# A fused attention and gated feed-forward kernel on one core: another written order of its pieces, with other pages and banks, behind an unchanged front part

## The chip, the cores and the metric

The kernel runs on one core of a Trainium2 chip. The metric is the device time of one execution in microseconds, the median over several runs. The core has five engines with a queue of instructions each: PE multiplies matrices, DVE, ACT and POOL work on elements, and SP issues the transfers (DMA) between the chip's main memory and the core. Each engine takes its instructions in order. An instruction that waits for another engine or for a transfer holds up everything behind it in its own queue.

## The reference

Local tokens (8 batches of 512) attend to the 32 global tokens of their batch and to local tokens within 32 positions; global tokens attend to everything. The result, 4608 tokens of 512, goes through a norm and a gated feed-forward layer:

```python
out_g = sm(scale * q_g @ k_all.T) @ v_all                      # 8 x 8 heads, 32 queries, 544 keys
s_ll  = where(|i - j| <= 32, scale * q_l @ k_l.T, -1e9)        # 512 x 512 for each head
out_l = sm([scale * q_l @ k_g.T, s_ll]) @ v_all
x  = concat(out_g, out_l)                                      # 4608 tokens x 512
xn = x / sqrt(mean(x * x) + 1e-6) * rms_g
y  = (silu(xn @ w_gate) * (xn @ w_val)) @ w_out                # 512 -> 1536 -> 512
```

## The kernel before

**Tiles and stages.** Tokens are done in nine chunks, c = 0 to 8: eight of 512 tokens, the last one of 256. Each chunk has an attention stage (pieces L, V, S, M, E, N, F, D, T, A and those with a G in front for the global tokens), a norm (n) and the feed-forward products. A product of 32-bit values is made of 16-bit high and low parts, as three matmuls. From chunk 1 on, the products in front of the gate use a scheme of seven products in place of eight: `moe_pair(ch, g, parts, n)` forms group g, six groups to a chunk. Its products stand as pieces P0 to P41, P(7g) to P(7g+6) for group g, and each is 12 matmuls of 256 columns. Piece R with the same number (`rest`) takes the sum out of its PSUM bank: on DVE as `tensor_tensor` (bank plus an earlier part), or on ACT as a copy. Several products of a group add on to one bank (`onto`), so R must have read the bank before the next product adds to it: P6 adds to the bank that R3 reads, and P2 begins a bank of its own. Two R pieces fill one tile, `u`: R4 on ACT and R5 on DVE. The pieces t form the gate, `moe_out` forms the products behind it (O0 to O41) and their R pieces from R49 on, and the stores.

**Weights.** They are prepared once by chunk 0 and put into main memory (`wd`, `wa`, `wb`). Every chunk fetches them again in pieces w: `fetch(c, g, i)` brings up to 512 KB from `wd` for two of the seven products, and `fetch_out` brings `wa` or `wb` for O.

**What sets the order.** Nothing is scheduled at build time. Every instruction is recorded under a piece name, "chunk:step.number", and at the end the pieces are written out in the order of a table. The queue of each of the five engines is this order with the other engines' pieces left out. Every instruction is issued from line 2095 (in `Later`), so all rows of the profile have that line:

```python
    for name in ORDER.split() or list(plan):
        for call in plan.pop(name):
            call()
```

Two more tables, `PAGES` and `BANKS`, give the place of each tile: 43 pages of 128 x 1024 words (and 8 wide ones) and 8 PSUM banks, taken one after the other in the order in which the program asks for tiles.

```python
        at = next(page_at)            # tile_of: the next word of PAGES, "25a" = page 25, first quarter
        return banks[int(next(bank_at))]   # bank_of
```

A tile may only be written when everything that used its page before has finished; the waits for this are put in from the places. So a table with other places has other waits, even between instructions that stay where they were.

Of the kernel before, what the change touches and what calls it, by code (L numbers as in the profile page):

```python
# [92 lines left out]
0:e3.5 0:M5.0.2 0:I4.11.0 0:p5.0 0:I4.01.0 0:e5.3 0:M5.0.1 0:m12.1 0:e5.0 0:g11.0 0:b3.0 0:M5.1.1
0:q10.0 0:B4.0 0:d6.0 0:e5.4 0:g11.1 0:e5.1 0:I5.00.0 0:I5.01.0 0:m17.0 0:m15.0 0:b4.0 0:I5.10.0
0:B5.0 0:s12.0 0:a8.0 0:e5.2 0:I5.11.0 0:q11.0 0:W14.0 0:a9.0 0:s17.0 0:M5.1.3 0:l12.1 0:s15.0
0:d8.0 0:e4.5 0:V5.0 0:I6.00.0 0:I6.01.0 0:B6.0 0:I6.10.0 0:l17.0 0:I7.10.0 0:h3.0 0:p6.0 0:l17.1
0:W16.0 0:e6.0 0:h4.0 0:l15.0 0:W13.0 0:m13.0 0:s13.0 0:k13.0 0:g13.0 0:e6.1 0:e6.2 0:g13.1 0:E5.1.0
0:b5.0 0:I6.11.0 0:I7.00.0 0:I7.01.0 0:d9.0 0:a10.0 0:B7.0 0:I8.10.0 0:d10.0 0:g17.0 0:E4.0.0
# [23 lines left out]
1:N0/0+1.0 1:w0.4 1:w14.0 1:P5.0 1:M0/0+1.0 1:N2/0+1.0 1:N3/0+1.1 1:N1/0+1.0 1:w2.0 1:N3/0+1.0
1:F3/0+1.0 0:J1.1 1:M2/0+1.0 1:R5.0 1:N0/0+1.1 1:GL/1+1.0 1:N2/0+1.1 1:M1/0+1.1 1:N1/0+1.1 1:R9.0
1:D3/0+1.0 1:R6.0 1:D3/0+1.1 1:P6.0 1:P7.0 1:P16.0 1:P2.0 1:M1/0+1.0 1:E2/0+1.0 1:P10.0 1:E1/0+1.0
1:F1/0+1.0 1:E0/0+1.0 0:o3.0 1:R10.0 1:P14.0 1:w3.0 0:u0.0 1:P12.0 1:F2/0+1.0 1:T3/0+1.0 1:w5.0
1:w6.4 1:D2/0+1.0 1:P11.0 1:D1/0+1.0 1:R7.0 1:P3.0 1:D1/0+1.1 1:w8.0 1:P18.0 1:w9.0 1:F0/0+1.0
1:D0/0+1.0 1:R3.0 1:P17.0 1:T1/0+1.0 1:D2/0+1.1 1:T2/0+1.0 0:J1.2 1:D0/0+1.1 1:T0/0+1.0 1:R17.0
1:R18.0 1:w11.0 1:R8.0 1:P19.0 1:P13.0 0:J1.4 1:A/0+1.0 1:B/0+1.0 1:R19.0 1:R4.0 0:j1.0 1:P15.0
0:u1.0 1:R5.1 1:w24.1 1:w24.2 1:R13.0 1:P26.0 1:w24.4 1:w30.0 1:X/0+1.0 1:w1.0 1:R20.0 1:Y/0+1.1
1:w30.1 1:R14.0 1:w30.3 1:P32.0 1:P33.0 1:R15.0 1:R11.0 1:w24.3 1:w46.0 1:w15.0 1:GS/1+1.0  # L130
1:GM/1+1.0 1:w26.0 1:GM/1+1.1 1:Y/0+1.0 1:Y/0+1.2 1:w38.0 1:w17.0 1:R33.0 1:GN/1+1.0 1:P24.0
1:GN/1+1.1 1:GM/1+1.2 1:GN/1+1.2 1:P25.0 0:o2.1 1:P20.0 1:R25.0 1:w30.2 1:w30.4 1:R16.0 1:P27.0
1:w46.1 1:w46.3 1:P21.0 1:GT/1+1.2 1:P40.0 1:P41.0 1:w32.0 1:X/0+1.1 1:R34.0 1:R17.1 1:w33.0 1:R26.0
1:R21.1 1:R41.0 1:GT/1+1.0 1:R27.0 1:X/0+1.2 1:GT/1+1.3 0:o3.1 1:P22.0 1:w18.0 1:GT/1+1.1 1:L/2+1.0
1:R42.0 1:P28.0 1:S/2+1.0 1:w48.1 1:N0/2+1.0 1:M1/2+1.0 1:N1/2+1.1 1:N1/2+1.0 1:P34.0 1:M3/2+1.1
1:M1/2+1.1 1:w38.1 1:w38.2 1:E1/2+1.0 1:F1/2+1.0 1:V/2+1.0 1:M2/2+1.0 1:w46.2 1:M2/2+1.1 1:E2/2+1.0
1:w46.4 1:w38.4 1:Y/0+1.3 1:M0/2+1.0 1:R21.0 1:N3/2+1.0 1:N2/2+1.0 1:N3/2+1.1 1:w38.3 1:M0/2+1.1
1:w18.1 1:E0/2+1.0 1:N0/2+1.1 1:F0/2+1.0 1:R9.1 1:w27.0 2:GL/1+1.0 1:P29.0 2:w18.1 1:R29.0
1:M3/2+1.0 1:E3/2+1.0 1:F3/2+1.0 2:w18.2 1:P23.0 1:w18.2 1:w18.4 1:D0/2+1.0 1:P35.0 1:R30.0 1:P30.0
1:P66.0 1:P31.0 1:R22.0 1:P38.0 1:w29.0 1:P39.0 1:P42.0 1:N2/2+1.1 1:P43.0 1:P36.0 2:GV/1+1.0  # L140
1:R12.0 1:D3/2+1.0 1:GA/1+1.0 1:D0/2+1.1 1:R28.0 1:w18.3 1:R23.0 1:D3/2+1.1 1:T3/2+1.0 1:P37.0
1:F2/2+1.0 1:w20.0 1:R31.0 1:w21.0 1:R24.0 1:T0/2+1.0 1:R13.1 1:D1/2+1.0 1:P46.0 2:w20.1 1:w44.0
1:w46.5 1:D1/2+1.1 3:w4.0 1:w40.0 1:D2/2+1.0 1:GN/1+1.3 1:w41.0 1:R35.0 1:R37.0 1:R25.1 1:D2/2+1.1
1:R29.1 1:R43.0 1:R36.0 0:o1.1 1:R37.1 1:w42.0 1:P44.0 1:L/0+2.0 1:R38.0 1:R39.0 1:w48.0 1:P47.0
1:R40.0 1:R41.1 1:T2/2+1.0 1:w43.0 1:R32.0 1:T1/2+1.0 1:A/2+1.0 1:w49.0 1:w23.0 1:w45.0 2:w0.0
# [2190 lines left out]
```

## Time and profile before

| | |
|---|---|
| time, median of 3 runs | 891.72 us (890.53 to 891.75) |
| the profiled execution's own time | 892.29 us |
| its span in the trace | 890.5 us (1.8 us lie around it) |
| busy: PE, DVE, ACT, POOL | 97%, 80%, 63%, 31% of the span |
| PE in the chain that ended last | 85% |

PE is busy nearly all the time. Its idle time by stages, the waits in which it lies, and the time by which other engines and transfers are ahead of it are what is to be read in this profile.

### The profile page before, as it was taken

The numbers are of one execution on the slowest core, as the hardware profiler recorded it, in microseconds if no ns is written. First come the engines' busy times: TensorE is split into PE (matmuls) and PEld (weight loads), VectorE is DVE, ScalarE is ACT, GpSimd is POOL, SyncE is SP. The second block draws the span as 40 slices with busy tenths as digits, with TensorE's granted clock in tenths as the row PEclk, the third lists the DMA queues.
The fourth block names the chain that finished last, engine by engine and source line by source line (L and its number), as shares of the span: only waits on it lengthen the run. The fifth ranks groups of instructions, "written<-read, shape, count | busy, mean of one in ns | idle before, by whom it ended". The sixth has DMA issues, their size and how long they took to land.

```text
span 890.5 us, 28310 instructions
## 1 busy us (share of the span) xinstructions
PE 864.1 (97%) x11646; PEld 666.4 (75%) x11646; DVE 709.7 (80%) x1857; ACT 557.9 (63%) x1362; POOL 277.8 (31%) x255
## 2 busy tenths in 40 slices
PE   5599999999999999999999999999999999999998
PEld 4554455545548885588888888888888888888997
DVE  5999999798686776777886899688886798587576
ACT  6999993657344664557473876568575772545343
POOL 0000000024834475414531255123441344124414
PEclk9699999999999999999999999999999999999999
DMA  9995340488974997984697567968796759747671
GB/s 353 407 392 190 96 142 25 141 277 283 374 253 143 288 304 230 312 266 150 218 376 263 172 224 218 339 234 291 254 366 206 253 152 366 262 140 229 229 255 62
DMA packets 102737, 216.79 MB, mean 243 GB/s; under 512 B 8272, under 2 KB 34640, under 8 KB 102608
## 3 DMA queue, kind: packets, MB, share of 16 engines
q1 hardware_dynamic: 102176, 214.66, 70.9%
q8 instruction: 91, 1.49, 0.7%
q10 hardware_dynamic: 432, 0.33, 0.1%
q14 instruction: 38, 0.31, 0.1%
HBM read 187.96 MB, written 27.00 MB: 241 GB/s over the span
## 4 chain that ended last, share of the span: by engine, by line
PE 85%; DMA 3%; DVE 3%; issue 1%; ACT 1%; SPq 1%; POOL 0%; DVEq 0%; POOLq 0%; ACTq 0%
PE bank L2095 85%; DVE page L2095 3%; DMA wide<-wd 1%; DMA page<-in_vb_dram 1%; DMA page<-in_gv_dram 1%; ACT page L2095 1%; DMA wb<-page 1%; SPq L2095 1%; POOL page L2095 0%; DVE wide L2095 0%; DVE xg L2095 0%; DVE ws L2095 0%; DVE sm L2095 0%; DVE hs L2095 0%; DVE pow L2095 0%
## 5 line engine op out<-in xcount | busy, mean ns | idle before, releaser
L2095 PE MATMUL bank<-page,page 128*128 128x256 f16 (+7 forms) x8406 | 726.8, 277 | 16.4 <-ACT page L2095 8.0
L2095 PEld LDWEIGHTS <-page 128*128 128x128 f16 (+1 forms) x5568 | 515.7, 98 | 159.4 <-issue 7.6
L2095 POOL TENSOR_TENSOR page<-page,page 128x512 f16<-128x512 f32 (+5 forms) x163 | 180.0, 1122 | 286.4 <-ACT page L2095 236.1
L2095 DVE TENSOR_TENSOR page<-bank,page 128x512 f32<-128x512 f32 (+1 forms) x179 | 113.9, 649 | 64.2 <-PE bank L2095 37.5
L2095 ACT COPY page<-bank 128x512 f32<-128x512 f32 (+3 forms) x172 | 86.9, 529 | 111.2 <-PE bank L2095 100.0
L2095 ACT CAST page<-page 128x512 f16<-128x512 f32 (+2 forms) x144 | 109.0, 780 | 73.5 <-DVE page L2095 59.9
L2095 ACT ACTIVATE page<-page,sm 128x128 f32<-128x128 f32 x344 | 126.5, 391 | 26.7 <-DVE sm L2095 21.7
L2095 DVE TENSOR_TENSOR page<-page,page 128x256 f32<-128x256 f32 (+4 forms) x145 | 90.5, 636 | 9.0 <-ACT page L2095 7.0
L2095 POOL TENSOR_TENSOR page<-page,sm 128x512 f32<-128x512 f32 x22 | 25.5, 1167 | 208.9 <-DVE sm L2095 201.0
L2095 ACT ACTIVATE page<-page 128x512 f32<-128x512 f32 (+2 forms) x93 | 77.1, 907 | 9.6 <-DVE page L2095 7.2
L2095 DVE CUSTOM_DVE_ANT_0 page<-bank,page 128x128 f32<-128x128 f32 x248 | 60.3, 283 | 19.9 <-PE bank L2095 18.8
L2095 PEld LDWEIGHTS bank<-page,page 64*32 64x32 f32 (+4 forms) x3072 | 55.2, 113 | 24.5 <-issue 11.0
L2095 PE MATMUL bank<-wide,page 32*64 32x96 f32 (+6 forms) x2074 | 63.4, 266 | 1.3 <-DMA page<-in_vb_dram 1.3
L2095 ACT ACTIVATE page<-page,half_inv 128x512 f32<-128x512 f32 (+1 forms) x68 | 44.7, 686 | 23.9 <-DVE page L2095 19.3
L2095 DVE TENSOR_TENSOR page<-page 128x256 f32<-128x256 f32 (+3 forms) x110 | 57.1, 533 | 1.1 <-PE bank L2095 0.2
L2095 PE MATMUL bank<-page,wide 128*128 128x256 f16 (+4 forms) x500 | 56.9, 269 | 0.8 <-DMA wide<-wd 0.8
L2095 DVE SCALAR_TENSOR_TENSOR page<-page,page 128x512 f32<-128x512 f32 (+1 forms) x68 | 46.8, 702 | 12.7 <-ACT page L2095 12.7
L2095 DVE SCALAR_TENSOR_TENSOR page<-page,c_h,page 128x512 f32<-128x512 f32 (+1 forms) x73 | 51.8, 728 | 0.7
L2095 PEld LDWEIGHTS <-wide 128*128 128x128 f16 x450 | 41.6, 98 | 13.9 <-DMA wide<-wd 1.1
L2095 ACT ACTIVATION_READ_ACCUMULATOR page<-page,sm 128x1 f32 x248 | 46.8, 189 | 0.0
L2095 POOL TENSOR_TENSOR page<-wide,page 128x512 f16<-128x512 f32 (+2 forms) x25 | 27.4, 1105 | 45.4 <-ACT page L2095 43.3
L2095 PEld LDWEIGHTS bank<-wide,page 32*64 32x64 f32 (+2 forms) x1936 | 29.5, 129 | 6.8 <-issue 2.7
(156 smaller groups left out, 662.1 us busy)
## 6 DMA issues: line engine op xcount, KB each, us to landing
page<-wd SPq DMA_DIRECT2D x117, 512.0 KB, 6.9
page<-wb SPq DMA_DIRECT2D x36, 512.0 KB, 7.0
page<-in_w_in_dram SPq DMA_DIRECT2D x24, 512.0 KB, 9.3
page<-wa SPq DMA_DIRECT2D x23, 512.0 KB, 6.4
page<-wd SPq DMA_DIRECT2D x42, 256.0 KB, 5.3
page<-in_qkb_dram SPq DMA_DIRECT2D x23, 448.0 KB, 6.1
wide<-in_gkq_dram SPq DMA_DIRECT2D x16, 576.0 KB, 8.1
page<-in_vw_dram SPq DMA_DIRECT2D x16, 512.0 KB, 9.3
```

What stands on the lines that cost most here:

```text
L2095: return lambda *a, **k: write(self.engine, lambda: call(*a, **k))
```

## The change

Only the three tables change. The 3754 pieces and the instructions in them are the same. Of `ORDER` the first 261 pieces stay, and 3376 of the others stand in another position (the median piece moves by 10 positions). Of the 1198 entries in `PAGES` the first 51 are as they were and 1079 differ; of the 438 in `BANKS` the first 40 are as they were and 346 differ. By the trace of before, the first instruction that stands elsewhere comes on SP at 56.5 us, on PE at 61.4, on DVE at 62.6, on ACT at 63.4 and on POOL at 181.

```diff
 ORDER = """
...
-0:d3.0 0:p4.0 0:W15.0 0:s8.0 0:e4.0 0:e4.1 0:g8.1 0:e3.1 0:I2.10.0 0:l8.0 0:g8.0 0:b1.0 0:e1.5
...
-0:S5.0 0:m10.0 0:d4.0 0:I3.00.0 0:I3.10.0 0:a7.0 0:q9.0 0:h2.0 0:I3.11.0 0:M5.1.2 0:a5.0 0:e4.4
...
 PAGES = """
...
-17a 18a 10a 21a 14a 22a 11a 0a 13a 20a 9a 1a 17a 3c 16a 12a 9a 14a 19a 32c 10a 39a 33a 8a 32c 15a
+17a 18a 10a 21a 14a 22a 11a 0a 13a 20a 9a 1a 17a 3c 16a 12a 9a 14a 19a 32c 10a 23a 42a 8a 32c 15a
...
```

**Place 1: chunk 7, group 0, from P4 to P6.** In the lists below a row is an instruction: what it writes, an arrow, what it reads, and the elements. The second number in a name is only a running one: `page25_88` is page 25. DVE before: these are R15, R2, R8, R3, R9 and R5.

```order
L2095 TENSOR_TENSOR page8_71<-bank1_115,page8_71 128x512
L2095 TENSOR_TENSOR page42_105<-bank7_121,page42_105 128x512
L2095 TENSOR_TENSOR page29_92<-bank6_120,page29_92 128x512
L2095 TENSOR_TENSOR page6_69<-bank0_114,page42_105 128x2x256
L2095 TENSOR_TENSOR page13_76<-bank3_117,page13_76 128x512
L2095 TENSOR_TENSOR page11_74<-bank7_121,page33_96 128x2x256
```

DVE now: R15, R9, then R5 (page 25), R3 and R6's sum as one row (x2), and t7.

```order
L2095 TENSOR_TENSOR page34_97<-bank3_117,page34_97 128x512
L2095 TENSOR_TENSOR page39_102<-bank0_114,page39_102 128x512
L2095 TENSOR_TENSOR page25_88<-bank1_115,page7_70 128x2x256
L2095 TENSOR_TENSOR page0_63<-bank6_120,page1_64 128x2x256 x2
L2095 SCALAR_TENSOR_TENSOR page9_72<-page9_72,page25_88 128x512
```

PE now, at the same place: the last matmuls of P4 (weights in page 25) and the first of P6 (bank 6).

```order
L2095 LDWEIGHTS page25_88
L2095 MATMUL bank7_121<-page8_71,page25_88 128x256
L2095 LDWEIGHTS page25_88
L2095 MATMUL bank7_121<-page30_93,page25_88 128x256
L2095 LDWEIGHTS page31_94
L2095 MATMUL bank6_120<-page35_98,page31_94 128x256
```

The tile `u`, which R5 writes, has moved from page 11 to page 25, which holds the weights of P4 and P5; and R3, which reads the bank of P6 (bank 0 before, bank 6 now), has moved from two places ahead of R5 to the place behind it. P4 stands directly ahead of P6, as it did before.

**Place 2: the start of chunk 7, from P7 to P2.** PE's pieces there were P8 P0 P1 P14 P2 P9 P15 P3 P7 and are P1 P8 P0 P7 P15 P14 P2 P9. ACT before: two casts and the copy R8 (of bank 6), three casts, R1 (of bank 5), the exponentials of the global attention, two copies, and R7 last (of bank 4).

```order
L2095 COPY page13_76<-bank6_120 128x512
L2095 CAST page16_79<-page15_78 128x512
L2095 CAST page5_68<-page11_74 128x512
L2095 CAST page15_78<-page36_99 128x512
L2095 COPY page42_105<-bank5_119 128x512
L2095 ACTIVATE wide2_108,gsm6_53_214<-wide2_108,gsm6_53_214 128x544 x2
L2095 ACTIVATE gsm6_53_214<-gsm6_53_214 128x2
L2095 COPY page33_96<-bank0_114 128x512
L2095 COPY page8_71<-bank2_116 128x512
L2095 COPY page29_92<-bank4_118 128x512
```

ACT now: an exponential, R7 (of bank 4, the product P7), the second exponential and its sum, a cast, and R8 (of bank 2).

```order
L2095 ACTIVATE wide1_107,gsm6_53_214<-wide1_107,gsm6_53_214 128x544
L2095 COPY page41_104<-bank4_118 128x512
L2095 ACTIVATE wide1_107,gsm6_53_214<-wide1_107,gsm6_53_214 128x544
L2095 ACTIVATE gsm6_53_214<-gsm6_53_214 128x2
L2095 CAST page9_72<-page20_83 128x512
L2095 COPY page39_102<-bank2_116 128x512
```

DVE now: R8's sum (page 41 with bank 2) stands ahead of the norm piece 6:n52.0, which writes page 8, read by P2.

```order
L2095 ISA wide1_107,gsm6_53_214<-bank3_117,zeros_130,gsm6_53_214 128x272
L2095 ISA gsm6_53_214 128x1
L2095 TENSOR_TENSOR page41_104<-bank2_116,page41_104 128x512
L2095 TENSOR_TENSOR page8_71<-page34_97,page9_72 128x512
L2095 TENSOR_TENSOR page1_64<-bank1_115,page1_64 128x512
L2095 TENSOR_TENSOR page7_70<-bank7_121,page7_70 128x512
```

On both engines the copy and the sum of group 1 (R7 and R8) have moved ahead of what P2 needs; before, R8's sum came behind the norm's pieces and behind P2's own result.

**Place 3: chunk 6, the weights of P23.** SP before: 6:w13 is the fifth row, into page 17, with a store ahead of it.

```order
L2095 DMA page2_65<-wd2_154 128x2048
L2095 DMA page21_84<-wd3_155 128x2x1024
L2095 DMA page18_81<-wd4_156 128x2048
L2095 DMA out_0_dram<-wide3_109 128x2x512
L2095 DMA page17_80<-wd3_155 128x2x1024
L2095 DMA page14_77<-wd3_155 128x2x1024
```

SP now: 6:w13 is the fifth row, into page 18.

```order
L2095 DMA page4_67<-wd4_156 128x2x1024
L2095 DMA page10_73<-wd5_157 128x1024
L2095 DMA page33_96<-wd4_156 128x2048
L2095 DMA page37_100<-wa_158 128x2048
L2095 DMA page18_81<-wd3_155 128x2x1024
L2095 DMA page20_83<-wd3_155 128x2x1024
```

PE now: the last matmuls of 6:P18 read page 18, and S/2+1 (64 matmuls of 128 columns), P22 and P20 stand between them and 6:P23, which reads page 18 again.

```order
L2095 LDWEIGHTS page18_81
L2095 MATMUL bank0_114<-page6_69,page18_81 128x256
L2095 LDWEIGHTS page18_81
L2095 MATMUL bank0_114<-page6_69,page18_81 128x256
L2095 MATMUL bank5_119<-page20_83,page9_72 32x128
L2095 MATMUL bank7_121<-page20_83,page9_72 32x128
```

The transfer of P23's weights now has the page that P18 reads until shortly before; before, it had page 17, and the trace issued it at 670.6 us, where P23 began at 700.1.

## Rows read from the trace of the kernel before

**Rows 1.** The page's line of busy time by engine, and its line of the chain that ended last, by engine.

```profile
PE 864.1 (97%) x11646; PEld 666.4 (75%) x11646; DVE 709.7 (80%) x1857; ACT 557.9 (63%) x1362; POOL 277.8 (31%) x255
PE 85%; DMA 3%; DVE 3%; issue 1%; ACT 1%; SPq 1%; POOL 0%; DVEq 0%; POOLq 0%; ACTq 0%
```

**Rows 2.** Busy time of each engine in stretches of the span: from and to, the length, PE, weight loads, DVE, ACT, POOL (number of instructions), then PE's granted clock as a share of full speed, the busy share of the DMA engines, and GB/s.

```profile
50.00:75.00 25.00, 23.77 (x198) 11.48 (x197) 24.83 (x67) 24.90 (x43) 0.00 (x0) 1.00 1.00 382
75.00:125.00 50.00, 50.00 (x448) 25.50 (x447) 49.12 (x122) 49.77 (x97) 0.00 (x0) 1.00 0.40 129
125.00:175.00 50.00, 50.00 (x551) 27.52 (x550) 44.05 (x120) 28.36 (x73) 0.87 (x1) 1.00 0.21 64
175.00:300.00 125.00, 124.78 (x1626) 74.07 (x1624) 97.03 (x245) 64.28 (x178) 58.29 (x46) 1.00 0.81 264
300.00:325.00 25.00, 24.20 (x290) 21.32 (x289) 19.61 (x56) 19.27 (x58) 13.98 (x10) 1.00 0.91 298
...
375.00:400.00 25.00, 24.49 (x449) 21.81 (x452) 18.63 (x36) 13.84 (x26) 2.60 (x3) 1.00 0.85 270
...
425.00:450.00 25.00, 23.66 (x459) 20.70 (x459) 21.01 (x55) 12.72 (x19) 11.57 (x11) 1.00 0.78 262
450.00:600.00 150.00, 149.88 (x2218) 131.66 (x2217) 121.92 (x317) 99.97 (x270) 45.29 (x41) 1.00 0.76 259
600.00:700.00 100.00, 99.79 (x1561) 87.59 (x1559) 78.44 (x213) 67.17 (x179) 36.92 (x34) 1.00 0.79 271
...
775.00:875.00 100.00, 99.91 (x1319) 91.62 (x1317) 75.39 (x178) 50.07 (x98) 33.98 (x38) 1.00 0.61 205
875.00:890.50 15.50, 11.70 (x104) 9.72 (x101) 6.78 (x18) 2.97 (x6) 8.12 (x15) 0.98 0.18 69
```

**Rows 3.** PE in order of time at two places: start, length, instructions, and in brackets the idle time ahead with its releaser.

```profile
65.77 1.46 PE L2095 MATMUL bank<-page,page 64*32 64x128 f32 x63 [0.68 <-DVE page L2095]
433.65 1.09 PE L2095 MATMUL bank<-wide,page 32*64 32x256 f32 x46 [1.34 <-DMA page<-in_vb_dram]
```

**Rows 4.** The chain that ended last, in order of time: start, length, what.

```profile
301.45 8.02 DMA wide<-wd
309.52 66.64 PE bank L2095 x765
376.18 0.59 ACT page L2095
376.87 0.69 DVE page L2095
...
425.96 7.55 DMA page<-in_vb_dram
...
603.89 0.59 ACT page L2095
604.51 0.70 DVE page L2095
605.25 28.54 PE bank L2095 x429
...
875.93 10.95 PE bank L2095 x98
886.89 0.02 issue
886.91 0.48 DVE page L2095
```

**Rows 5.** PE and then DVE in order of time at place 1, columns as in rows 3.

```profile
762.76 9.44 PE L2095 MATMUL bank<-page,page 128*128 128x256 f16 x85
...
767.62 2.48 DVE L2095 TENSOR_TENSOR page<-bank,page 128x512 f32<-128x512 f32 x4 [1.88 <-ACT page L2095]
```

**Rows 6.** ACT in order of time at place 2.

```profile
757.06 1.66 ACT L2095 CAST page<-page 128x512 f16<-128x512 f32 x3
759.14 0.59 ACT L2095 COPY page<-bank 128x512 f32<-128x512 f32 x1 [0.42 <-PE bank L2095]
759.62 0.75 ACT L2095 ACTIVATE wide<-wide,gsm 128x544 f32<-128x544 f32 x1
760.27 0.19 ACT L2095 ACTIVATION_READ_ACCUMULATOR wide<-wide,gsm 128x1 f32 x1
760.36 0.74 ACT L2095 ACTIVATE wide<-wide,gsm 128x544 f32<-128x544 f32 x1
761.00 0.19 ACT L2095 ACTIVATION_READ_ACCUMULATOR wide<-wide,gsm 128x1 f32 x1
761.23 0.21 ACT L2095 ACTIVATE gsm<-gsm 128x2 f32<-128x2 f32 x1
761.34 1.05 ACT L2095 COPY page<-bank 128x512 f32<-128x512 f32 x2
```

**Rows 7.** Transfers: number, KB each, and the median us from issue to landing; over the whole span, then of those issued between 668 and 674 us, then between 690 and 700 us.

```profile
page<-wd SPq DMA_DIRECT2D x117, 512.0 KB, 6.9
page<-wb SPq DMA_DIRECT2D x36, 512.0 KB, 7.0
...
page<-wd SPq DMA_DIRECT2D x4, 512.0 KB, 7.6
...
page<-wd SPq DMA_DIRECT2D x1, 512.0 KB, 3.8
```

**Rows 8.** Two stretches in front of the change, columns as in rows 2.

```profile
15.00:25.00 10.00, 6.90 (x144) 4.60 (x145) 9.13 (x36) 9.90 (x43) 0.00 (x0) 0.72 1.03 411
25.00:45.00 20.00, 12.56 (x254) 11.69 (x254) 18.39 (x52) 18.75 (x28) 0.00 (x0) 0.71 1.03 406
```

More of the change, by code (lines that the diff above doesn't have):

```diff
@@ L93 @@
[L93 to L98, printed above, removed]
@@ L122 @@
[L122 to L127, printed above, removed]
@@ L128 @@
[L128 to L145, printed above, removed]
@@ L388 @@
[L388 to L393 removed]
+0:d3.0 0:W15.0 0:L6.0 0:s8.0 0:m11.1 0:l8.0 0:e3.1 0:I2.10.0 0:p4.0 0:e4.0 0:s11.0 0:s9.0 0:g8.1
@@ new lines @@
+1:N2/0+1.0 0:J1.4 1:w11.0 1:N3/0+1.0 1:E3/0+1.0 1:E0/0+1.0 1:P14.0 1:P2.0 0:u2.0 1:M2/0+1.0
+1:F3/0+1.0 1:w30.1 1:D3/0+1.0 1:P3.0 0:J1.3 1:P18.0 1:E2/0+1.0 1:D1/0+1.0 1:F2/0+1.0 1:D3/0+1.1
+1:R10.0 1:P19.0 1:w3.0 1:R7.0 1:D1/0+1.1 1:N0/0+1.0 1:F0/0+1.0 1:P12.0 1:w30.2 1:R3.0 1:P13.0
+1:R11.0 1:P15.0 1:D0/0+1.0 1:D0/0+1.1 1:D2/0+1.0 1:w14.0 1:D2/0+1.1 1:R18.0 1:R8.0 1:w5.0 1:R13.0
+1:T0/0+1.0 1:T2/0+1.0 1:T1/0+1.0 1:T3/0+1.0 1:A/0+1.0 1:B/0+1.0 1:P32.0 1:R14.0 1:P33.0 0:j1.0
+0:u1.0 1:Y/0+1.0 1:P24.0 1:P25.0 1:R19.0 1:R9.1 2:w18.1 1:R15.0 1:R12.0 1:w15.0 1:R20.0 1:R21.1
@@ new lines @@
+2:R13.0 2:S/2+1.0 2:P17.0 2:M2/2+1.1 2:t16.0 2:R16.1 2:N0/2+1.0 2:M2/2+1.0 1:GX/1+1.0 2:P18.0
+2:M1/2+1.0 2:M0/2+1.1 2:R16.0 1:GX/1+1.1 2:N2/2+1.1 2:t14.0 2:N2/2+1.0 2:E2/2+1.0 2:N0/2+1.1 2:w27.0
+2:F2/2+1.0 2:M1/2+1.1 2:t15.1 2:w29.4 2:M3/2+1.1 2:M3/2+1.0 2:E3/2+1.0 2:P19.0 3:w6.0 2:R17.0
+2:t17.0 2:w31.1 2:P21.0 2:w32.0 1:R53.1 2:P22.0 2:R19.0 2:w47.0 2:R22.0 2:R21.0 2:P23.0 2:N3/2+1.0
+2:P25.0 2:w18.0 2:R23.1 2:P20.0 2:P24.0 2:N3/2+1.1 2:R18.0 2:w47.1 2:R23.0 2:P26.0 2:N1/2+1.0
+2:P28.0 2:R20.1 2:R20.0 2:P35.0 2:N1/2+1.1 2:t21.0 2:R20.2 2:E1/2+1.0 2:w17.0 2:t18.0 3:w59.0
@@ new lines @@
+4:N1/2+1.0 4:t14.1 4:M0/2+1.1 4:t16.1 4:t15.1 4:M2/2+1.1 4:t16.0 4:P18.0 4:F3/2+1.0 4:P22.0
+4:D3/2+1.0 4:E1/2+1.0 4:P28.0 4:D3/2+1.1 4:P16.0 4:E0/2+1.0 4:M2/2+1.0 4:P21.0 4:w38.0 4:E2/2+1.0
+4:R16.0 4:P19.0 4:R18.0 4:Y/0+1.3 4:N0/2+1.0 4:R17.0 4:t17.0 4:t17.1 4:t9.1 4:w10.0 4:P36.0 4:P20.0
+4:R28.0 4:t16.2 4:w48.0 4:w20.0 4:N2/2+1.0 4:t17.3 4:GV/1+1.0 4:T3/2+1.0 4:R19.0 4:R21.0 4:R22.0
+4:P23.0 4:t9.2 4:P24.0 4:t9.0 4:GN/1+1.3 4:F0/2+1.0 4:N2/2+1.1 4:t10.0 4:t10.1 4:R23.0 4:R20.0
+4:t10.2 4:w24.0 4:P31.0 4:P29.0 4:t10.3 4:R20.2 4:t21.0 4:R20.1 4:t21.1 4:t22.1 4:t22.0 4:P26.0
@@ new lines @@
+7:O0.0 7:t11.0 7:R12.0 7:R11.0 7:P22.0 7:P16.0 7:R13.0 7:R10.0 7:w13.0 7:R15.0 7:R16.0 7:R13.1
+7:t14.1 7:P13.0 7:t12.0 7:t14.0 7:O1.0 7:O2.0 7:P18.0 7:t10.3 7:R18.0 7:R13.2 7:t15.0 7:t15.1
+7:t16.1 7:t16.0 7:P19.0 7:t17.0 7:t17.1 7:t16.2 7:P23.0 7:R17.0 7:w40.0 7:P20.0 7:R19.0 7:w48.0
+7:R22.0 7:t17.2 7:R23.0 7:t18.0 7:t19.0 7:w50.0 7:O3.0 7:R20.1 7:R20.2 7:t21.1 7:w22.0 7:O5.0 7:O4.0
+7:P21.0 7:R20.0 7:t21.0 7:t22.0 7:R21.0 7:t22.1 7:w36.0 7:t23.0 7:t24.0 7:t23.1 7:t24.1 7:R22.1
+7:w31.0 7:t23.2 7:t24.2 7:P26.0 7:t25.0 7:P24.0 7:R24.0 7:P25.0 7:R25.0 7:R26.0 7:R27.1 7:w61.0
```

641 lines of the change are left out of this document (324 added, 317 removed), and 18 rows, old and new, of the table BANKS.

## The prediction

> **What bounds the kernel now.** I read the busy time by engine first and then the chain that ended last [rows 1]: PE is busy 97% of the span and holds 85% of the chain. An average over stages says little, so next come the stretches [rows 2]. Behind 75 us PE is busy in whole stretches (50.00 of 50, 124.78 of 125, 149.88 of 150). Busy is here the same as working at full rate: at place 1, 85 matmuls of 256 columns take 9.44 us [rows 5], 0.111 us each, and a piece of 12 takes 1.31 us at a granted clock of 1.00. The change neither adds nor takes away a matmul, so all that it can win are the gaps. From 50 us up to 875 us the lengths less PE's busy time in [rows 2] give 1.23 + 0.22 + 0.80 + 0.51 + 1.34 + 0.12 + 0.21 + 0.09 = 4.5 us. Behind 875 us another 3.8 us are idle: the last matmuls, one DVE piece and the last store [rows 4], which end the program in the same way now. In front of 50 us the order is as it was.
>
> [...]
>
> **What the change removes.** The gaps have names. At 65.8 us S5 waits 0.68 for DVE, and at 433.7 the attention of chunk 3 waits 1.34 for its values [rows 3], a transfer of 7.55 us in the chain [rows 4]; another of 8.02 ends at 309.5, and at 376 a sum on ACT and DVE is late. S5 now stands some twenty pieces later, and the others have other pages and neighbours. I let all 4.5 us go: bounds 2.5 (only the four named stretches gain, and half of the first comes back) and 4.5.
>
> **What it puts in their place.** At every matmul that waits for another engine or a transfer I compared, in the new order, PE's work since the releasing instruction with the time the released chain needs, with the durations of the same instructions in the trace. Most have microseconds to spare. These have not:
>
> *A. P4 to P6 in chunk 7 (place 1).* R5 writes page 25 and must wait until P4, which reads its weights there, has ended. R3 stands behind R5 on DVE, and P6, next on PE, adds to the bank that R3 reads. So PE stands from P4's end through two DVE sums. Four such sums take 2.48 us [rows 5], 0.62 each: 1.24, and a release at either end. The chain at 603.89, one ACT copy and one DVE sum between two matmuls, took 1.36 [rows 4]. Bounds 1.3 and 1.5; I take 1.4. Before, R3 had no such instruction ahead of it, and P6 ran on without a gap [rows 5].
>
> *B. P7 to P2 in chunk 7 (place 2).* P2 reads page 8, which 6:n52.0 on DVE writes; ahead of it is R8's sum, which waits for ACT up to R8's copy. Behind P7's end ACT does R7 (half of 1.05: 0.53), an exponential with its sum (760.36 to 761.34: 0.98), a cast (a third of 1.66: 0.55), R8 (0.53) [rows 6]; then DVE does two sums (1.24): 3.83. PE has P15 and P14 in between, 2.62. That leaves 1.2; bounds 1.1 and 1.4 (releases).
>
> *C. P23 in chunk 6 (place 3).* The fetch can start only when P18 has ended. Until P23 PE has two pieces (2.62) and 64 attention matmuls (63 took 1.46 [rows 3]): 4.1 us, and 4.5 by the starts of the same pieces before. A 512 KB fetch lands in 6.9 in the median, 7.6 a little earlier in this chunk, 3.8 in the one case nearest by time [rows 7]. Bounds 0 and 3.5; I take 1.5, since the nearest row is the short one.
>
> *D. 3:P2 at 368 us.* Its weights (2:w58) are issued behind five stores of 2:w53, which wait for POOL; some 7.5 us of PE's work lie between: 0 to 2.4, I take 0.7.
>
> *E. The front.* DVE is busy 24.83 of 25 us and 49.12 of 50 [rows 2], so what it owes PE there is not made faster by another order: with S5 away, I3.10 at 67 us comes 2 us of PE's work earlier and waits for DVE itself, 0.5 to 0.9. Two more waits, 1:P0 at 158 us and 1:A/0+1 at 187, hang on DVE's whole backlog: 0 to 2.8 together. I take 1.7 of 0.5 to 3.7.
>
> *F. Fetches with 6 to 8 us.* Those for 3:P34, 7:O8, 7:O18 and 4:P19 (this one waits for a store to leave its page) land in time or within a few tenths at 6.9 [rows 7], and up to 1.4 late each where they meet others, as the 8.02 and 7.55 us ones did [rows 4]: 0 to 5.6 for the four; I take 1.5.
>
> *G. Small waits* at 2:P25, 3:P25, 3:O12, 5:P39, 6:O13, 7:GX and 8:P26, where the sum from a bank comes about when it is needed: 0.2 to 0.7 each by whether the sums take 0.62 or run one behind another. 1.3 to 5.0; I take 2.5.
>
> The other engines' work is the same in kind and number, and none becomes a bound behind 175 us: DVE has 97 of 125 us there, and less later [rows 2].
>
> **The sum.** 1.4 + 1.2 + 1.5 + 0.7 + 1.7 + 1.5 + 2.5 = 10.5 new, less 4.5: +6.0. The profiled execution took 892.29 (span 890.5, and 1.8 around it), 0.6 above the median of the runs, within their spread. 892.3 + 6.0 = **898.3 us**. With all low ends: 1.3 + 1.1 + 0.5 + 1.3 = 4.2, less 4.5: 892.0. With all high ends and only 2.5 removed: 23.1 - 2.5 = +20.6, 913.
>
> **Rivals.** 0.2% (1.8 us) is about what a measurement of this kernel can tell from no change.
>
> *No difference*: the low ends hold, new gaps replace old ones, 891 to 893.5. For it: half of C to G is decided by some tenths of a microsecond on transfers whose landing I can't know. Against it: A and B alone are 2.6, and need nothing to go badly.
>
> *Faster*: the load of the transfers decides. Fetches that come at other times meet less traffic and land in about 4 us, as the one at 690 to 700 did [rows 7]. It decides from 4.1 us downward, at C, and above that at D and F, which then cost nothing; with DVE's sums at 0.62 E and G nearly vanish. Left are A and B: 892.3 - 4.5 + 2.6 = 890.4, just 0.2% faster. Against it: DMA is busy 0.76 to 0.91 of the stretches from 300 us to 600 [rows 2], and the bytes are the same.
>
> *The transfers lead the other way*: as many fetches meet, each of C, D and F at its high end: 3.5 + 2.4 + 5.6 with A, B, E and G as taken, 18.3 - 4.5: 906. For it: the medians of 6.9 and 7.0 [rows 7] are at or above most of those leads.
>
> [...]
>
> **How the numbers follow.** My forecast (894 to 903, its own range) has 0.63, no difference 0.13, faster 0.08, transfers 0.13, clock 0.03. The predicted time is that of the forecast, 898. From 893 to 907 the range leaves out the faster case, most of no difference, and the clock. Slower by over 0.2%: 0.80; within 0.2%: 0.12; faster by over 0.2%: 0.08.
>
> **What would show it.** Right: in the trace of the changed kernel PE waits 1.2 to 1.6 us for DVE twice between 755 and 775 us, where [rows 5] has no gap; a wait for a transfer from `wd` near 695; no wait for the values near 433 and none at S5. PE's busy time stays at 864, and its idle time behind 50 us, the tail apart, is 8 to 14 us. Wrong: if R3 or n52.0 do not hold PE at those places, my reading of the waits by page and bank fails, and A and B go. If PE's gaps there are as I say and the time is still 892, the gaps elsewhere are hidden, and C to G were too high. If PE's busy time moves by over 1 us, the mix of matmuls on PE matters, which I hold to be unchanged.

## The result, and the profile after

The changed kernel takes 904.26 us (median of 4 runs, 903.66 to 904.84) where the kernel before, run on the same chip, takes 891.74 (890.53 to 892.77): 1.0141 times as long, interval 1.0123 to 1.0158. It is slower, as forecast, but by 12.5 us instead of 6. The profiled execution took 903.66 us, its span is 901.9.

The page's lines of busy time and of the chain that ended last, after; they answer to [rows 1]:

```profile
PE 866.6 (96%) x11646; PEld 667.3 (74%) x11646; DVE 715.7 (79%) x1857; ACT 557.2 (62%) x1362; POOL 279.9 (31%) x255
PE 78%; DVE 9%; ACT 3%; issue 2%; DMA 2%; POOL 0%; DVEq 0%; ACTq 0%; POOLq 0%; SPq 0%
```

Two numbers moved that I had held to be fixed: with the same instructions PE is busy 2.5 us longer and DVE 6.0 us longer. In the chain DVE has gained what PE and DMA lost.

Busy time by stretches after, columns as in [rows 2]:

```profile
50.00:75.00 25.00, 24.11 (x144) 11.58 (x143) 24.55 (x62) 25.00 (x35) 0.00 (x0) 1.00 1.00 386
...
175.00:300.00 125.00, 123.17 (x1611) 72.46 (x1610) 94.84 (x241) 65.63 (x180) 64.13 (x48) 1.00 0.87 272
...
425.00:450.00 25.00, 23.97 (x534) 21.07 (x534) 21.87 (x48) 11.75 (x21) 9.32 (x9) 1.00 0.88 310
450.00:600.00 150.00, 148.06 (x2086) 129.40 (x2084) 119.99 (x303) 97.62 (x260) 47.77 (x42) 1.00 0.74 246
600.00:700.00 100.00, 96.80 (x1526) 83.89 (x1524) 81.74 (x211) 65.84 (x173) 33.48 (x31) 1.00 0.73 247
700.00:750.00 50.00, 49.14 (x719) 42.89 (x717) 41.14 (x106) 34.11 (x86) 18.83 (x16) 1.00 0.82 259
750.00:775.00 25.00, 23.76 (x219) 21.15 (x217) 16.72 (x28) 9.20 (x20) 7.74 (x8) 1.00 1.03 360
775.00:875.00 100.00, 98.31 (x1235) 89.05 (x1232) 71.34 (x162) 45.86 (x88) 28.03 (x29) 1.00 0.65 212
```

PE's granted clock is 1.00 throughout, so the clock is no part of it. The idle time is spread: 1.83 us before 300, 1.94 from 450 to 600 (0.12 before), 3.20 from 600 to 700 (0.21 before), 1.24 and 1.69 in chunk 7.

PE's waits from 50 us on, after: engine and what it writes, what it waited for, then us in total, times, the longest.

```profile
PE bank L2095 <- DVE page L2095: 6.6, 10, 1.5
PE bank L2095 <- issue: 4.2, 4, 1.8
PE bank L2095 <- ACT page L2095: 1.6, 4, 0.8
PE bank L2095 <- POOL page L2095: 0.6, 3, 0.3
PE bank L2095 <- DVE nt L2095: 0.6, 2, 0.3
```

No transfer stands here, so nothing that I had priced on fetches happened. The waits for DVE are more than A and B. And four waits of 4.2 us have "issue" as releaser: PE stood, and no engine or transfer that the profile knows of let it go.

PE in order of time at the four places (start, length, instructions, idle ahead with its releaser):

```profile
255.02 2.12 PE L2095 MATMUL bank<-page,page 128*128 128x512 f16 x9 [1.81 <-issue]
393.86 0.82 PE L2095 MATMUL bank<-page,page 128*128 128x256 f16 x6 [0.68 <-issue]
440.60 1.16 PE L2095 MATMUL bank<-wide,page 64*32 64x128 f32 x64 [1.03 <-issue]
737.41 0.81 PE L2095 MATMUL bank<-page,page 128*128 128x256 f16 x6 [0.70 <-issue]
```

They lie inside pieces (in the middle of 1:P70, 3:P13, 3:S/0+2 and 6:P41), where nothing new is waited for.

### The profile page after: what moved, and what is told of

Read it like the earlier page. It is cut to its first block, busy times and chain, and to the rows that moved or that the text cites. A ratio compares the mean times of both kernels' runs of the same rounds, so it can differ in the third digit from the quotient of the medians.

```text
span 901.9 us, 28355 instructions
## 1 busy us (share of the span) xinstructions
PE 866.6 (96%) x11646; PEld 667.3 (74%) x11646; DVE 715.7 (79%) x1857; ACT 557.2 (62%) x1362; POOL 279.9 (31%) x255
## 4 chain that ended last, share of the span: by engine, by line
PE 78%; DVE 9%; ACT 3%; issue 2%; DMA 2%; POOL 0%; DVEq 0%; ACTq 0%; POOLq 0%; SPq 0%
PE bank L2095 78%; DVE page L2095 7%; ACT page L2095 3%; DMA page<-wd 1%; DVE wide L2095 1%; DVE nt L2095 0%; DMA page<-in_gv_dram 0%; POOL page L2095 0%; DVE xg L2095 0%; ACT wide L2095 0%; ACT sm L2095 0%; DVE sm L2095 0%; DVE hs L2095 0%; DVE gsm L2095 0%; DVEq L2095 0%
## 5 line engine op out<-in xcount | busy, mean ns | idle before, releaser
L2095 PE MATMUL bank<-page,page 128*128 128x256 f16 (+7 forms) x8448 | 742.3, 279 | 24.9 <-ACT page L2095 9.8
L2095 POOL TENSOR_TENSOR page<-page,page 128x512 f16<-128x512 f32 (+5 forms) x176 | 195.0, 1127 | 375.2 <-ACT page L2095 332.8
L2095 ACT CAST page<-page 128x512 f16<-128x512 f32 (+2 forms) x155 | 119.2, 792 | 113.4 <-DVE page L2095 102.6
L2095 DVE TENSOR_TENSOR page<-page,page 128x256 f32<-128x256 f32 (+5 forms) x164 | 102.2, 634 | 10.0 <-ACT page L2095 8.7
L2095 PEld LDWEIGHTS bank<-page,page 64*32 64x32 f32 (+4 forms) x3072 | 55.8, 115 | 22.7 <-issue 10.5
L2095 DVE TENSOR_TENSOR page<-page 128x256 f32<-128x256 f32 (+3 forms) x127 | 64.9, 529 | 4.6 <-POOL page L2095 3.5
L2095 ACT ACTIVATE page<-page,half_inv 128x512 f32<-128x512 f32 (+1 forms) x73 | 48.0, 683 | 18.3 <-DVE page L2095 16.9
L2095 DVE SCALAR_TENSOR_TENSOR page<-page,page 128x512 f32<-128x512 f32 (+1 forms) x73 | 52.3, 729 | 8.6 <-ACT page L2095 8.3
L2095 PE MATMUL bank<-wide,page 32*64 32x96 f32 (+8 forms) x1900 | 53.3, 263 | 1.0 <-issue 1.0
L2095 PE MATMUL bank<-page,wide 128*128 128x256 f16 (+2 forms) x414 | 52.7, 276 | 1.2 <-DVE page L2095 1.2
L2095 PEld LDWEIGHTS bank<-wide,page 32*64 32x64 f32 (+3 forms) x1792 | 29.7, 128 | 6.7 <-issue 4.3
L2095 DVE STREAM_TRANSPOSE wide<-page 128x512 f32<-128x512 f32 x46 | 31.0, 692 | 2.5 <-POOL page L2095 2.0
```

Source lines behind the costliest of these rows:

```text
L2095: return lambda *a, **k: write(self.engine, lambda: call(*a, **k))
```

## The ledger of the gaps

Idle time leaves out what a waiting matmul is booked as busy. So I went through PE's starts instead: for each pair of neighbours, by how much the second starts later than the same two do back to back. Behind 56 us this gives 6.7 us before and 16.9 after, 10.1 of the 11.4 us by which the span grew; about 1 us had come by 47 us, where the two orders are still the same, and is the difference of two executions. The named gaps, worked out from the two traces:

```
gone    3:A/2 (values) 1.94, 0:S5 1.06, 2:P28 0.97, 0:p4 0.71, 3:P15 0.68, seven of 0.25 to 0.34   7.4
new  A  7:P6 (P4's page, R5 ahead of R3)                                            1.63
     B  7:P2 (R8's sum ahead of n52)                                                1.40
     E  0:I3.10 (DVE's backlog)                                                     1.05
     G  2:P25 0.34, 3:P25 0.29, 5:P39 0.56, 7:O15 behind 7:GX 0.61                  1.80
     U  inside 1:P70 1.98, 3:P13 0.84, 3:S/0+2 1.29, 6:P41 0.86 ("issue")           4.97
     V  3:O15-O16 1.93, 4:O15-n44 0.85, 5:n44-O16 1.39, 6:P19 1.28                  5.45
     W  six others of 0.27 to 0.41                                                  2.0
     C, D, F                                                                        0.0
                                                                        sum of new 18.3
```

18.3 less 7.4 is 10.9; the small differences elsewhere make it 10.1. U and V, over half of what is new, have no term in the prediction.

**V.** DVE and then POOL at 6:P19, columns as above:

```profile
697.40 0.29 DVE L2095 TENSOR_TENSOR page<-bank,gsm 128x128 f32<-128x128 f32 x1
697.61 1.50 DVE L2095 TENSOR_TENSOR page<-page 128x256 f32<-128x256 f32 x1
699.03 1.47 DVE L2095 TENSOR_TENSOR page<-bank,page 128x512 f32<-128x512 f32 x2
...
696.37 3.27 POOL L2095 TENSOR_TENSOR page<-page,page 128x512 f16<-128x512 f32 x3 [8.11 <-ACT page L2095]
```

and PE there:

```profile
699.76 1.47 PE L2095 MATMUL bank<-page,page 128*128 128x256 f16 x12 [1.12 <-DVE page L2095]
```

The sum of 128x256 at 697.61 takes 1.50 us; this form takes 0.42 in the median when POOL does nothing. POOL's third piece runs from 697.57 to 698.83, and DVE's instruction ends 0.28 behind it. Behind it on DVE stands R16's sum, for which P19 waits. All four places of V have such a row (1.43 for 3:t44.3, 1.38 for 4:t38.1, 1.22 for 5:t46.0 instead of 0.69). By both traces it goes by which instructions meet, and which starts first (the times without a bracket are means):

```
after, DVE TENSOR_TENSOR 128x256, both inputs in pages:  160 without POOL 0.42 (at most 0.43), 31 beside it 0.68, up to 1.50
after, DVE TENSOR_TENSOR 128x512, one input in a bank:   96 without POOL 0.68 (at most 0.69), 83 beside it 0.68
DVE's instructions, their time over the median of their form, summed:  24.8 us before, 31.0 after
```

The 6.2 us more in the last row account for the 6.0 by which DVE's busy time grew. Of the 34 sums of 128x256 with no input in a bank that started while a piece of POOL ran, in the two traces, 32 ended 0.28 to 0.35 us behind it; the 38 that started ahead of such a piece and ran beside it took 0.39 to 0.43. By what means a piece of POOL holds DVE, the traces do not show. I had not asked of any DVE instruction what POOL does beside it.

**U.** The page of either kernel lists a queue beside the data's (packets, MB, share of the DMA engines):

```profile
q8 instruction: 91, 1.49, 0.7%
```

91 transfers of 16 KB for 23,292 matmuls and weight loads make 256 PE instructions each. I counted, at each of the four gaps, how many PE instructions had started when PE stood (matmuls, weight loads and the 84 semaphore and drain instructions of PE's queue): each time 193 more than a multiple of 256. And PE goes on 2.2 to 2.7 us after one of these transfers began. So what PE waits for in U is its own next block of instructions. That is a reading of four gaps; whether the block's limits make them, or the places in the work, is for experiments.

## The experiments

The rivals for the 6 us that were missed: the places A and B cost more than their gaps (T1); POOL holds DVE (V); instruction blocks (U). Against U stood that "issue" may be only a wait that the trace does not hold, bound to its place in the program.

**Two pieces back in front** (a wait's price by itself):

```diff
-7:P14.0 7:R0.0 7:R8.1 6:n52.0 7:P2.0
+7:P14.0 7:R0.0 6:n52.0 7:R8.1 7:P2.0
...
-7:P4.0 7:R4.0 7:R5.0 7:R3.0 7:R6.0
+7:P4.0 7:R3.0 7:R4.0 7:R5.0 7:R6.0
```

> The changed kernel with two pieces moved in the order: 7:R3 stands ahead of 7:R4 and R5, and 6:n52.0 ahead of 7:R8's sum. If the waits at A and B come from the queue order that the prediction named, the gaps of 1.63 us (ahead of 7:P6) and 1.40 us (inside 7:P2) are below 0.2 each, and the time falls by about 3.0 us, 904.3 to 901.3. If P6 and P2 wait for something else at these places (a page, a transfer), the gaps stay and the time is 903.5 to 905. The four gaps that the trace puts down to no releaser (at 255.0, 393.9, 440.6 and 737.4 us: 1.98, 0.84, 1.29 and 0.86) lie ahead of the edit: they stay at the same matmuls if they are set by the program, and are elsewhere or gone if they are chance.

Measured: 900.09 us (899.71 to 902.57), 1.0098 of before [1.0078, 1.0118], so 4.2 less than the changed kernel. PE at the two places and its waits from 50 us on (lines are 14 less, the table is shorter):

```profile
769.68 1.47 PE L2081 MATMUL bank<-page,wide 128*128 128x256 f16 x12
771.00 2.78 PE L2081 MATMUL bank<-page,page 128*128 128x256 f16 x24
773.62 1.47 PE L2081 MATMUL bank<-page,wide 128*128 128x256 f16 x12
774.93 5.29 PE L2081 MATMUL bank<-page,page 128*128 128x256 f16 x47
...
PE bank L2081 <- DVE page L2081: 4.4, 8, 1.1
PE bank L2081 <- issue: 2.8, 4, 1.5
```

Both gaps are gone, two DVE waits and 2.2 us fewer in the list. A and B are two instructions out of their place and 3.0 us; of the other 1.2, the four "issue" gaps, all of them ahead of the edit, give 1.5 (here they are 0.88, 0.52, 1.72 and 0.38 by the starts). Those come out otherwise from one execution to the next. So T1 falls: 8 us over before are left without A and B.

**POOL's pieces cut short** (fifteen pieces of chunks 3 to 6 beside which DVE was held; where they subtract they write zeros, otherwise they do 8 columns, so that part of the gate and of the attention's sums is left out):

```diff
+    def few(x):
+        if piece[0] not in FEW:
+            return x
+        return x[:, :8] if len(x.shape) == 2 else x[:, :, :8]
...
+            if self.engine == "gpsimd" and op == "tensor_tensor":
+                return lambda d, x, y, f: write(
+                    self.engine,
+                    lambda: now.gpsimd.memset(d, 0)
+                    if f == ALU.subtract and piece[0] in FEW
+                    else call(*map(few, (d, x, y)), f),
+                )
```

> The changed kernel with 15 POOL pieces cut short around six of PE's waits: sums in place over 8 columns, and low parts set to zero in place of a difference of two pages. Left out is that part of the sums of squares and of the low parts in chunks 3 to 6. Theory, POOL holds DVE: a DVE instruction that reads two pages and starts while a POOL sum runs lasts until POOL's has ended and 0.28 more (6:t16.1 took 1.50 us in place of 0.42, 3:t44.3 1.43, 4:t38.1 1.38). Then these take 0.42 to 0.75 again, and PE's gaps at 440 to 454 (3:O15 to O17, 1.9), 547 (0.85), 646 to 648 (1.4) and 699.8 (6:P19, 1.28) lose 3.5 to 5 us together: 899.5 to 901. Rival, the queue order alone makes these waits, and POOL only runs beside them: the gaps stay within 0.3 each, and the time is 903 to 905.

Measured: 899.35 us (898.74 to 900.27), 1.0082 [1.0063, 1.0100], 4.9 less than the changed kernel. Busy time by stretches, and PE's waits from 50 us on:

```profile
500.00:600.00 100.00, 100.00 (x1421) 88.25 (x1424) 82.82 (x203) 67.74 (x175) 31.81 (x31) 1.00 0.75 244
600.00:700.00 100.00, 98.62 (x1621) 86.25 (x1612) 78.84 (x210) 66.82 (x175) 29.18 (x32) 1.00 0.74 253
...
PE bank L2110 <- issue: 5.6, 4, 2.5
PE bank L2110 <- DVE page L2110: 4.8, 7, 1.5
```

DVE's sum of 128x256 at 6:P19, and a stretch behind the first "issue" gap:

```profile
694.59 0.44 DVE L2110 TENSOR_TENSOR page<-page 128x256 f32<-128x256 f32 x1
...
254.60:258.00 3.40, 3.31 (x8) 1.20 (x9) 3.37 (x14) 3.34 (x6) 2.41 (x2) 0.51 0.79 288
```

Of V's 5.45 us 5.0 are gone (0.43 of the 1.28 stays at 6:P19), and from 600 to 700 us 1.38 us are idle where 3.20 were. V is shown: DVE's instructions are the same, only their neighbours on POOL are shorter, and the four rows of V are back at 0.42, 0.42, 0.69 and 0.44 us. "issue" has grown again (the gap sum by starts is 6.3 in place of 5.0), with nothing changed near its first place, at 254.7 us. That takes back 1.4 of V's 5.0. The gap there is 2.70 us, and behind it the granted clock is 0.51 for some 3 us, which costs another 1.3: six matmuls of 512 columns start 0.43 us apart in place of 0.21.

**The blocks shifted.** A transpose piece of chunk 0, written out several times: 36 more PE instructions each time, far ahead of the places, nothing else moved. If PE waits for blocks, the gaps leave their places and come where the new limits fall; if the places make them, they stay. Five times is 144 instructions more, over half a block:

```diff
-        for call in plan.pop(name):
+        calls = plan.pop(name)
+        for call in calls * (5 if name == "0:p3.0" else 1):
             call()
```

> The changed kernel with 0:p3 (17 small matmuls at 58.5 us) written five times in place of once, just ahead of a wait for DVE that hides most of it. Nothing else is moved; PE's list of instructions is some 140 longer ahead of everything behind 60 us. Theory, PE's instructions come late: PE's list is fetched in blocks of 16 KB (91 such transfers in the trace), and PE stands from shortly behind the start of a late one until 2.3 to 2.7 us behind it. With other block limits the four gaps without a releaser (at 1:P70, 3:P13, 3:S/0+2 and 6:P41: 1.98, 0.84, 1.29, 0.86) vanish or move to other matmuls; the time changes by -4 to +2 us. Rival, something at these places holds PE: the gaps stay at the same matmuls, within 0.3 us, and the time is 904 to 906.5.

> The kernel before with 0:p3 written five times, as in the run above with the changed one. Theory, PE's instructions come late: the kernel before had next to no such gap by the places of its blocks, and with other limits it gets some of up to 2 us that have no releaser in the trace: 892 to 896. Rival, the gaps belong to the changed order: none appears here, and the time is 891.5 to 893.5 (the added matmuls take 2.8 us, 1.5 of which the waits at 61 and 66 us hide).

Measured: the changed kernel so shifted 923.42 us (922.39 to 925.21), 1.0356 of before [1.0336, 1.0376]; the kernel before so shifted 929.22 (924.03 to 930.23), 1.0407 [1.0374, 1.0441]. PE's waits, first of the changed kernel shifted, then of before shifted, which has no "issue" wait unshifted; and PE in order of time at some places, in the same order:

```profile
PE bank L2095 <- issue: 14.4, 6, 3.7
...
PE bank L2095 <- issue: 21.7, 9, 4.2
```

```profile
441.60 0.94 PE L2095 MATMUL bank<-page,page 128*128 128x256 f16 x7 [3.08 <-issue]
538.42 0.41 PE L2095 MATMUL bank<-wide,page 32*64 32x64 f32 x17 [3.75 <-issue]
...
242.15 5.38 PE L2095 MATMUL bank<-page,page 128*128 128x512 f16 x127 [1.96 <-issue]
546.75 1.86 PE L2095 MATMUL bank<-wide,page 32*64 32x32 f32 x22 [4.23 <-issue]
```

The gaps moved off the four places to others, and again PE stood each time at 193 instructions past a multiple of 256. That is what the theory expected of the places; both times lie far above what I expected, by 17 us (changed kernel) and by 33 (before). In the kernel before, with its order, pages and banks untouched, about 3 us of added work (PE's starts at 72 us, against those at 58) cost 37.5 us. 25.5 of them are the gaps at block limits by the starts. The rest is about what the granted clock says:

```profile
500.00:600.00 100.00, 92.80 (x1367) 80.50 (x1366) 77.37 (x194) 61.22 (x166) 32.47 (x29) 0.95 0.67 215
...
700.00:800.00 100.00, 93.21 (x1198) 80.76 (x1185) 70.00 (x162) 54.35 (x125) 31.06 (x29) 0.95 0.66 228
```

The clock records of before and after hold two levels alone, 0.50 (16.2 to 19.4 us, before) and 1.00 (50 to 889). With these, 0.95 over 100 us is 10 us at the low one, 5 us lost in each stretch (the estimate takes PE as busy in them). In this run the clock fell to the low level at six of the ten gaps at limits, of 2.2 to 4.4 us each; at one of 2.7 us (363.2) it did not, nor in the changed kernel shifted at one of 3.2 (441.6). Behind the gaps up to 2 us of the changed kernel it did not.

**Shifted by nearly a whole block, and by a little.** 252 instructions more put the limits 4 away from where they were, 36 more put them elsewhere:

```diff
-        for call in calls * (5 if name == "0:p3.0" else 1):
+        for call in calls * (8 if name == "0:p3.0" else 1):     # 252 more, before and after
...
+        for call in calls * (2 if name == "0:p3.0" else 1):     # 36 more, before
```

> The kernel before with 0:p3 written eight times: 252 more instructions on PE in front of 60 us, nearly a whole block of 256, where four more copies (144 instructions) cost 37 us. Theory, PE's instructions come in blocks: every later block limit is again where it was in the kernel before, four instructions apart, so no gap at a limit appears, and only the added matmuls cost: 7 x 0.68 = 4.8 us less what the waits at 61 and 66 us hide (1.5 to 2.5): 894 to 895.5. Rival, more matmuls at this place cost for another reason (the clock, a late start of the front): with more copies it costs more than the 37 us, 930 to 960.

> The kernel before with 0:p3 written twice: 36 more instructions on PE. Theory, blocks: by the times of the kernel before, with each limit 36 instructions earlier and the fetch starting 0.8 us (DMA idle) to 3.8 us (DMA busy) behind the first use of the block ahead and 2.45 us long, the gaps add up to 9 us: 899 to 903. Rival: one copy costs a quarter of the 37 us or less only by chance; without the block limits it costs at most the 0.7 us of its matmuls: 891.5 to 892.5.

> The changed kernel with 0:p3 written eight times (252 more instructions on PE). Theory, blocks: limits as in the changed kernel, four instructions apart: the four gaps without a releaser stay at 1:P70, 3:P13, 3:S/0+2 and 6:P41 and sum to 3.5 to 6.5; the time is 904.3 + 4.8 - 1.0 to 2.0 hidden: 907 to 908.5, where 144 more took 923.4. Rival, as in the run above: over 925.

Measured: before with 252 more 897.56 (897.03 to 899.37), 1.0062 [1.0047, 1.0078]; before with 36 more 903.07 (898.84 to 904.86), 1.0111 [1.0084, 1.0137]; the changed kernel with 252 more 909.46 (908.28 to 910.22), 1.0191 [1.0176, 1.0206]. So the kernel before pays 11.4 us for 36 instructions and 5.9 for 252. PE's "issue" waits with 252 more, with 36 more, and the changed kernel with 252 more:

```profile
PE bank L2095 <- issue: 0.9, 1, 0.9
...
PE bank L2095 <- issue: 7.4, 7, 2.0
...
PE bank L2095 <- issue: 2.5, 4, 0.8
```

The kernel before with 252 more: PE behind the added copies, and the stretch there:

```profile
64.72 4.76 PE L2095 MATMUL bank<-page,page 128*128 128x512 f16 x12
...
62.00:69.00 7.00, 7.00 (x77) 4.29 (x74) 3.90 (x15) 3.11 (x6) 0.00 (x0) 0.51 0.64 254
```

What decides is where the limits fall, not the work added. With 36 more, eight limits of 0.3 us and more make 8.9 of the 11.4 by the starts. With 252 more one gap of 1.07 at 442.4 is at a limit, just behind the place where the wait for the values [rows 3] is 1.34 shorter than before; so the 5.9 are the price of the added copies (PE's starts at 72 us are 5.9 later, against those at 58). The changed kernel rises by 5.2, and its four gaps are back, each 5.5 to 6 us later than it was: 0.85 at 261.0, 1.00 at 399.9, 1.06 at 446.2, 0.37 at 742.9, together 3.3 where I expected 3.5 to 6.5. Both kernels went slightly over the times that I expected, because the copies cost more than their own matmuls: while they run the clock falls to the low level, and the twelve matmuls of 512 columns behind them take 4.76 us, some 2 more than at 0.21 each. No gap is ahead of the fall; PE was busy all the time, with the copies' matmuls of 1 or 2 columns.

**Three waits of before removed** (each a piece moved ahead, for a version that beats both):

```diff
-2:w22.0 ... 2:w18.0
+2:w18.0 2:w22.0
-3:R1.1 3:w25.0 3:P3.0 3:GN/1+1.0
+3:GN/1+1.0 3:R1.1 3:w25.0 3:P3.0
-4:w55.0 ... 3:V/2+1.0
+3:V/2+1.0 4:w55.0
```

> The kernel before with three pieces moved, none of them on PE: 3:V/2+1 (two transfers) ahead of the fetch 4:w55, the fetch 2:w18 ahead of 2:w22 and a store, and 3:GN/1+1.0 on DVE ahead of 3:R1's sum. If PE's gaps before are set by what the trace names, those at 433.7 (1.94 us), 309.5 (0.97) and 378.0 (0.68) shrink to 0.3 and less, and the time falls by 2.5 to 3.3 us to 888.4 to 889.2. Rival, something else comes due next (other transfers that now land later, POOL against DVE): the gaps move, and the time is 890.5 to 892.5.

Measured: 890.98 (889.94 to 893.97, 12 runs) against 891.70 (17 runs) of before, 0.999 [0.998, 1.000]: at the edge of what can be told, and 2 us short of what was expected; the rival, that the gaps move, had 890.5 to 892.5. The three waits are gone, and where the longest of them was, PE stands again:

```profile
432.83 0.76 PE L2081 MATMUL bank<-wide,page 32*64 32x96 f32 x49 [0.84 <-issue]
```

A block's limit (193 past a multiple of 256) falls there. That the 1.34 us of waiting for the values [rows 3] had given this block its time fits; no run tests it by itself.

**When a limit costs.** From the six traces of before, after and the first four experiments, for 494 limits. On the left the time in which PE ran the 284 instructions ahead of the limit, whether it then stood over 0.4 us, and the mean over all limits of the row. On the right the delay from the first of these 284 to the start of the transfer (hardly any began sooner), by how busy the data's queue kept the DMA engines.

```
284 ran in            limits   stood   mean us      DMA busy     limits   delay us: median, 9 of 10 below
under 4 us                18      13      1.89      under 0.3        85   0.7, 1.3
4 to 5                    11       3      0.58      0.3 to 0.7       96   1.2, 2.6
5 to 6                    27      10      0.60      0.7 to 0.95     112   2.6, 4.6
6 to 7                    49       2      0.05      over 0.95       201   3.4, 5.4 (longest 10.1)
over 7                   389       1      0.05
```

The transfer began hardly ever sooner than about one block ahead, in the median 0.7 us behind that with the DMA engines under 0.3 busy and 3.4 with them over 0.95; where PE stood, it went on 2.2 to 2.8 us after the transfer's start. In pieces of 12 matmuls of 256 columns (24 instructions in 1.31 us) 284 instructions last 15.5 us by estimate, and over 7 us PE stood at one limit of 389; in attention, 63 matmuls and their weight loads in 1.46 us [rows 3], they last 3.3 us, and under 4 us it stood at 13 of 18.

## Why the prediction was right and where it was wrong

- **A** was right: PE stands from P4's end, through R5 and R3 on DVE, until P6: 1.47 us idle (1.4 forecast). **B** was right: 1.24 (1.2). PE and DVE at both places, after:

```profile
771.04 0.27 PE L2095 MATMUL bank<-page,wide 128*128 128x256 f16 x1
772.55 1.36 PE L2095 MATMUL bank<-page,wide 128*128 128x256 f16 x11 [1.24 <-DVE page L2095]
...
777.68 1.47 PE L2095 MATMUL bank<-page,page 128*128 128x256 f16 x12
780.62 1.58 PE L2095 MATMUL bank<-page,page 128*128 128x256 f16 x13 [1.47 <-DVE page L2095]
...
771.21 0.69 DVE L2095 TENSOR_TENSOR page<-bank,page 128x512 f32<-128x512 f32 x1 [4.33 <-ACT page L2095]
771.81 0.68 DVE L2095 TENSOR_TENSOR page<-page,page 128x512 f16<-128x512 f32 x1
...
779.19 1.29 DVE L2095 TENSOR_TENSOR page<-bank,page 128x512 f32<-128x512 f32 x2 [1.50 <-PE bank L2095]
```

  On DVE R8's sum and n52 stand ahead of P2, R5 and R3 ahead of P6. By the starts they are 1.63 and 1.40, 0.2 more each, which was to be added to any price taken from an idle row. That these two gaps are only an order of two instructions was shown by moving them. They stand at 772.6 and 780.6 us, the second behind the stretch of 755 to 775 that I named, since the kernel is late by then.
- **C** cost nothing. The fetch was issued at 702.57 and P23 came 4.5 us later, as worked out; it landed in 3.7, about the 3.8 that [rows 7] had for the nearest fetch. PE's 4.60 us there have no idle time, the wait for `wd` near 695 that I gave as a sign did not come, and the range's low end held. What the DMA queue shows for fetches issued from 702.4 to 703:

```profile
page<-wd SPq DMA_DIRECT2D x1, 512.0 KB, 3.7
```

- **D** and **F** cost nothing either: PE's list of waits has no transfer. Of 3.7 us for C, D and F together none came. The value that I took lay between the ends each time, where the low end was the right one.
- **E** was 1.05 of 1.7, at 0:I3.10 alone; 1:P0 and 1:A/0+1 run on.
- **G**: of the seven places four stand, 1.80 us of 2.5.
- **What goes** was 7.4 us instead of 4.5. My sum came from busy time, and a wait of which part is booked inside a matmul is larger by the starts (3:A/2 1.94 where the row has 1.34 idle). The same lies behind PE's busy time: "it stays at 864" was wrong by 2.5, but not since the mix of matmuls moved: with the order of the changed kernel kept and POOL shortened it is 865.2, and with two pieces moved 865.4. It goes up and down with the gaps, as far as these runs tell.
- **The step that failed** is the comparison "at every matmul that waits for another engine or a transfer", with the durations of the same instructions in the trace. It left out U and V, 10.4 us, for two reasons. The durations of DVE were those beside the old neighbours on POOL (V, 5.45, and part of W). And a matmul that waits for no engine and no transfer can still wait, for its own instructions (U, 4.97). "None becomes a bound behind 175 us" was true of shares and beside the point: the waits are of single instructions.

By these terms: +6.0 forecast, new gaps 18.3 in place of 10.5, gaps gone 7.4 in place of 4.5, which is +10.9; with about 1 us of the two executions it gives about the 11.4 between the profiled ones. That the kernel is slower at all is not owed to the terms that I had: A to G as measured are 5.9 new, less the 7.4 gone, -1.5. The direction that I forecast came from U, V and W, which I did not have: that part was luck.

PE's idle time behind 50 us, the tail apart, is 13.7 us and so inside the 8 to 14 that I gave as a sign, but mostly by other waits than those named.

Of the rivals, "no difference" and "faster" asked that the fetches cost nothing, which came true; A and B were in both. "Faster" had 890.4, about what A to G as measured give, and lost by what had no term. "The transfers lead the other way" gave 906 and so was nearest in time, for a reason of which the trace shows nothing. Only the list of waits tells it apart: it has no wait for a fetch. The transfers do have a part, which no rival had, since the blocks come late where the data's queue is dense (3.4 us in the median, against 0.7). The clock, with 0.03, did not fall behind 50 us in this kernel: it was 1.00 in every stretch from 50 to 875 us. Nor is it gaps alone that go with a low clock: in the run with 252 more it was 0.51 without one.

What stays open: why the transfer of a block does not begin earlier, and how much of the sizes of U is the density of the transfers and how much is chance (the same gap was 1.98, 0.88 and 2.70 in three kernels with the same order up to there). No kernel that holds the limits and thins the transfers was run. W was not tested by itself.

## What to carry to other kernels

When a written order is changed, look at two things beside the waits: the places where a run of tiny matmuls holds more than one block of 256 PE instructions under dense transfers (here 13 of 18 limits stood where 284 instructions ran in under 4 us), and the element-wise instructions on DVE that now run beside one of POOL with both inputs in SBUF (here up to 1.50 us in place of 0.42). Here 36 PE instructions more moved the limits behind them and cost 11.4 us, 144 more 37.5, and 252 more, which put them four instructions away, 5.9; so a control for an edit that adds or takes PE instructions adds nearly a whole block somewhere, with the clock behind it looked at, and a kernel that seems well tuned may be so by where its limits fall. Read PE's waits by their releaser before believing a time that fits.
